# Identity products on TensorE in the first ten slots, and the weights' conversion begun one slot earlier with its last six units late

## The chip, the cores and the metric

The kernel runs on one core of a Trainium2 chip. The metric is the device time of one execution in microseconds (us). The engines are named as in the profile: PE (TensorE: matrix products and transposes), DVE (VectorE), ACT (ScalarE), POOL (GpSimd) and SP (SyncE, which here only issues DMA transfers). Each engine works through its own queue in the order in which the program wrote it.

## The reference

Attention in which every row of scores keeps its 32 largest entries, followed by a two-layer MLP with an exact GELU:

```python
B, H, S, D = 8, 8, 576, 64
scores = q @ k.transpose(0, 1, 3, 2) / sqrt(D)
kth = np.partition(scores, -32, axis=-1)[..., -32:-31]
scores = np.where(scores >= kth, scores, -1e9)
attn = np.exp(scores - scores.max(-1, keepdims=True))
attn = attn / (attn.sum(-1, keepdims=True) + 1e-9)
o = attn @ v                                     # float32
x = o.transpose(0, 2, 1, 3).reshape(4608, 512)
h = x @ w_in                                     # 512 x 2048
out = (0.5 * h * (1 + erf(h / sqrt(2)))) @ w_out # 2048 x 512
```

q, k and v are float32. The weights w_in and w_out lie in memory as 64-bit floats, and the kernel converts them to 32-bit ones itself.

## The kernel before

**Items and slots.** The attention is cut into 144 items. An item is one tile of 128 query rows for a pair of heads (two rows of 576 scores for each partition), or the last 64 query rows of two pairs together. The loop over `n` (line 651) is a software pipeline; one pass of it is called a slot here. Slot `n` issues, in this order: the addition for the weights' unit of the slot (`weights_add`), the scores of item n+2 (`scores`, PE, copied by ACT), the product with v for item n-3 (`attend`, PE; it does something for every second item only), the softmax of item n-1 (ACT, four passes), the transposes of item n-2 (`transposes`: one piece of tails and two main pieces of four transposes, PE, each copied by ACT), the transposes of q and k of coming pairs (`transpose_qk`), the search of the 32 largest for item n (`top_k`, 14 passes of MAX8 and MATCH_REPLACE8 on DVE), the threshold of item n (`threshold`, POOL), the normalising of item n-1 (`normalise`, two passes of POOL or of DVE), the sizing of the next unit of weights (`weights_size`, ACT) and the loads for later slots (SP).

The sum of a softmax row (the denominator) passes from ACT to POOL (`add_small`, line 372) and then to DVE (`inverse`, line 366, at the end of the search of the next item). Its result is what `normalise` needs, and the transposes of the slot after need that.

**MLP.** Its work is cut into pieces (four passes each of 256 columns in the first layer, two of 512 in the second), and `mlp` strews them between the attention's work on PE, 8 in a slot. The first can be issued in slot START = 10, when the first 256 tokens have gone through the attention; slots 10 and 11 take 4 each, later slots 8. What is left after the last slot follows without attention.

**Weights.** There are 16 units of 2 x 128 rows by 512 columns. `load_weights` brings the 64-bit words of a unit with two transfers into a part of `w_out_sb` that is not yet in use, or into a tile of its own (`stage`, lines 154 to 158). `weights_size` makes two passes on ACT (lines 175 and 177) and a third (line 179) that POOL takes over (line 191) for units from slot 12 on; `weights_add` and `weights_end` add on POOL (lines 194 and 206). For units up to slot 10 the second addition stands late in the slot (`ends_late`), behind `add_small`. When a unit's third pass is POOL's, `normalise` goes to DVE in the slot before. Unit i of ORDER is in slot 1 + i, the last one in slot 17:

```python
SLOT_OF = {u: FIRST + i + (i == UNITS - 1) for i, u in enumerate(ORDER)}
```

**PSUM.** The scores have one buffer (`s_ps`). Transposes, the tails of scores and the product with v share a ring of two (`tp`), so PE can't start a piece before ACT has copied the one before the last. A product of zeros runs nine times ahead of the loop (line 630), into the ring of the MLP's first layer.

Of the kernel before, what the change touches and what calls it, by code (L numbers as in the profile page):

```python
# [14 lines left out]
def kernel(  # L15
# [19 lines left out]
    nc = tc.nc  # L35
    f32, i32, u32 = mybir.dt.float32, mybir.dt.int32, mybir.dt.uint32
# [5 lines left out]
    P = 128  # L42
# [19 lines left out]
    ps = ctx.enter_context(tc.tile_pool(name="ps", bufs=2, space=bass.MemoryType.PSUM))  # L62
    ctx.enter_context(tc.manual_schedule())

    ident = const.tile([P, P], f32, name="ident")
# [44 lines left out]
    UNITS = NWI + FT // 2  # L110
# [10 lines left out]


    ORDER = [0, 1, 2, 3, 8, 9, 4, 5, 10, 11, 6, 7, 12, 13, 14, 15]
    FIRST = 1
    START = 2 * NP + 2
    WARM = 9
    words = {}
# [3 lines left out]
    nc.gpsimd.memset(high, EXP0 * 2.0**-21)  # L131


    SLOT_OF = {u: FIRST + i + (i == UNITS - 1) for i, u in enumerate(ORDER)}
    UNIT_IN = {n: u for u, n in SLOT_OF.items()}
    unit_in = UNIT_IN.get

    def load_weights(n, queue=None):

        queue = queue or nc.sync  # L140
        u = unit_in(n)
        if u is None:
            return
        src, r, c, dst = weights_of(u)
        if src.dtype == f32:
            for x in range(2):
                queue.dma_start(
                    out=dst[:, x], in_=src[(r + x) * P : (r + x + 1) * P, c : c + WS]
                )
            return  # L150


        half, i = src.bitcast(u16), ORDER.index(u)
        if i not in (12, 14, 15):
            at = FT // 2 + 4 * (i % 2)
            t = w_out_sb[:, at : at + 4, :].rearrange("p (a b) n -> p a (b n)", a=2)
        else:
            t = stage.tile([P, 2, 2 * WS], f32, tag="words", name="words")
        for a in range(2):
            queue.dma_start(  # L160
                out=t[:, a].bitcast(u16)[:, 0 : 4 * WS - 1],
                in_=half[(r + a) * P : (r + a + 1) * P, 4 * c + 1 : 4 * (c + WS)],
            )
        words[u] = t
# [15 lines left out]

    def on_pool(u):

        return u in words and SLOT_OF[u] >= START + 2

    made = set()

    def weights_add(u):
        if u in words:
            w, _, below, d = parts(u)
            if on_pool(u):  # L190
                nc.gpsimd.tensor_scalar(
                    w.bitcast(i32), w.bitcast(u32), 2.0**-13, None, op0=ALU.mult
                )
            nc.gpsimd.tensor_tensor(d, d, below, op=ALU.add)
            if not ends_late(u):
                weights_end(u)
        made.add(u)

    def ends_late(u):

        return u in words and SLOT_OF[u] <= START

    def weights_end(u):
        if u in words:
            w, _, _, d = parts(u)
            nc.gpsimd.tensor_tensor(d, d, w.bitcast(i32), op=ALU.add)
# [66 lines left out]
    def scores(i):  # L273
        if i >= N:
            return
        pair, t = items[i]
        S_of[i] = s = work.tile([P, 2 * S], f32, tag="s", bufs=5, name="s")
        s_ps = ps.tile([P, 2, 512], f32, tag="s", bufs=1, name="s_ps")
        t_ps = ps.tile([P, 512], f32, tag="tp", name="t_ps")
        if t < NM:  # L280
            qk = qk_of[pair]
            lhsT = qk[:, t * P : (t + 1) * P]
            nc.tensor.matmul(t_ps[:, 0:P], lhsT=lhsT, rhs=qk[:, SM + P : KT], start=True, stop=True)  # L283
            for c in range(2):
                for e in range(2):
                    rows = slice(e * D, (e + 1) * D)
                    nc.tensor.matmul(  # L287
                        s_ps[:, e, c * 256 : (c + 1) * 256], lhsT=lhsT[rows, :],
                        rhs=qk[rows, KT + c * 256 : KT + (c + 1) * 256], start=True, stop=True,
                    )  # L290
            if i == 0:

                nc.scalar.activation(s[:, 0:SM], s_ps[:, 0], func=AF.Copy, scale=scale)  # L293
                nc.vector.tensor_scalar(s[:, SM : S + TL], t_ps[:, 0:P], scale, None, op0=ALU.mult)
                nc.scalar.activation(s[:, S + TL :], s_ps[:, 1], func=AF.Copy, scale=scale)  # L295
                return
            nc.scalar.activation(spread(s, S + TL, SM), s_ps, func=AF.Copy, scale=scale)  # L297
            nc.scalar.activation(s[:, SM : S + TL], t_ps[:, 0:P], func=AF.Copy, scale=scale)
        else:
            for r in range(2):  # L300
                qk = qk_of[pair + r]
                for e in range(2):
                    nc.tensor.matmul(
                        t_ps[half(r, e), r * TL : (r + 1) * TL],
                        lhsT=qk[:, SM + e * TL : SM + (e + 1) * TL],
                        rhs=qk[:, SM + P + e * TL : SM + P + (e + 1) * TL],
                        start=True, stop=True,
                    )

            for r in range(2):  # L310
                qk = qk_of[pair + r]
                for e in range(2):
                    rows = slice(e * D, (e + 1) * D)
                    nc.tensor.matmul(  # L314
                        s_ps[half(r, e), r, :], lhsT=qk[rows, SM + e * TL : SM + (e + 1) * TL],
                        rhs=qk[rows, KT:], start=True, stop=True,
                    )
            s2 = s.rearrange("p (r n) -> p r n", r=2)
            nc.scalar.activation(s2[:, :, 0:SM], s_ps, func=AF.Copy, scale=scale)
            nc.scalar.activation(  # L320
                s2[:, :, SM:S], t_ps[:, 0:P].rearrange("p (r n) -> p r n", r=2),
                func=AF.Copy, scale=scale,
            )
# [116 lines left out]
    def copy_x():  # L440
        while copies:
            copies.pop()()
# [161 lines left out]
    def mlp(n):  # L604
        for _ in range(n):
            if done[0] >= len(pieces) or pieces[done[0]][0] > ready[0] or left[0] == 0:
                return
            pieces[done[0]][1]()
            done[0] += 1
            left[0] -= 1  # L610
            if eager[0]:
                run_gelus()
# [8 lines left out]
    load("k", 1)  # L621
    load("q", 1)
    for n in range(2):
        load_weights(FIRST + n)


    idle = raws["v"][0][:, NM].rearrange("p e d -> p (e d)")
    warm = ps.tile([P, 512], f32, tag="l1", name="warm")
    for _ in range(WARM):
        nc.tensor.matmul(warm[:, 0:P], lhsT=idle, rhs=idle, start=True, stop=True)  # L630
    for pair in range(2):
        for piece in transpose_qk(pair, pair == 0):
            piece()
        if pair == 0:
            scores(0)
            scores(1)

# [11 lines left out]
    for n in range(ahead):  # L651

        left[0] = 4 if n in (START, START + 1) else 8
        eager[0] = n > N
        weights_add(unit_in(n))
        scores(n + 2)
        product = attend(n - 3)
        late = n > START
        if n <= START:

            softmax(n - 1, 0)
        copy_x()
        mlp(1)
        tr = transposes(n - 2)
        if product and n > START and done[0] < len(pieces) and pieces[done[0]][0] > ready[0]:

            for piece in tr[:1]:
                piece()
            tr, ready[0] = tr[1:], n_tok[0]
        if n > START:  # L670
            softmax(n - 1, 0)
        mlp(1)
        if not late:
            softmax(n - 1, 1)
        mlp(1)
        prep = prep_in.pop(n, [])
        if len(prep) > 1 and len(tr) == 3:
            tr, prep = tr[:1] + prep[:1] + tr[1:], prep[1:]
        for piece in tr[:-1]:
            piece()  # L680
            ready[0] = n_tok[0]
            mlp(1)
        ready[0] = n_tok[0]
        if late:
            softmax(n - 1, 1)
        add_small(n - 1)
        if ends_late(unit_in(n)):
            weights_end(unit_in(n))
        for piece in tr[-1:] + prep:
            piece()  # L690
            mlp(1)

        run_gelus()
        mlp(left[0])
        run_gelus()
        if n < N:
            top_k(n, {3: lambda: inverse(n - 1)})
        else:
            inverse(n - 1)
        threshold(n)  # L700
        u = unit_in(n + 1)

        normalise(n - 1, 2 if on_pool(u) else 0)

        weights_size(unit_in(n + 1))
        if n >= FIRST:
            load_weights(n + 2)
        if n <= NP:
            load("v", n)

# [37 lines left out]
```

## Time and profile before

| | |
|---|---|
| Median of 4 runs | 1641.33 us (1639.95 to 1642.26) |
| The profiled execution | 1641.79 us, its span 1640.0 us |
| Busy share of the span | PE 97%, DVE 86%, ACT 72%, POOL 40% |
| Granted PE clock, mean | 0.979 |
| First MAX8 of slots 0, 4, 9, 10, 11, 12 | 11.15, 49.92, 98.43, 108.13, 117.83, 130.16 us |
| DVE's search in one slot of the first ten | 9.7 us |
| DVE waiting for denominators, 108 to 260 us | 11.0 us in 9 waits |

How to read it: the span is the time from the first to the last instruction. The page gives busy time for each engine, and rows of tenths for 40 equal slices of the span (9 is 90% or more); its row PEclk has the share of the full PE clock that was granted. A line of a timeline has the start, the time taken, the engine, the line of the kernel, the operation, what it writes and reads, the count, and in brackets the idle time before it and what ended it. Passes of PE overlap, and the end of each is modelled, so the distance from one start to the next is a better price than the time taken.

### The profile page before, as it was taken

The page shows a single profiled execution, that of the slowest core. Times are in us where ns is not written, and L with a number is a line of the kernel's source. Part 1 is how long each engine was busy: PE and PEld are TensorE (multiplying, and loading weights), DVE is VectorE, ACT ScalarE, POOL GpSimd, SP SyncE. Part 2 cuts the span into 40 slices and gives each one's busy share as a digit, 9 for nine tenths or more (in the row PEclk, how much of TensorE's full clock was granted, in tenths as well). Part 3 has the DMA queues.
Part 4 walks back from the last instruction along what each step waited for, and adds up shares of the span by engine and source line. Part 5 has one row for each costly group of instructions (what it writes and reads, how often), then busy time and mean ns, then how long its engine had stood idle before and what let it go on. Part 6 is the DMA issues. An engine that isn't in the chain of part 4 may idle for free.

```text
span 1640.0 us, 25030 instructions
## 1 busy us (share of the span) xinstructions
PE 1589.4 (97%) x8818; PEld 1076.7 (66%) x8818; DVE 1415.2 (86%) x3046; ACT 1185.6 (72%) x2133; POOL 662.3 (40%) x759
## 2 busy tenths in 40 slices
PE   6669999999999999999999999999999999999999
PEld 4346576766666666676666667676666666666665
DVE  7998999988898989998989898998889888999800
ACT  6999877777777777777777777777777777777720
POOL 4897633333333333333333233333333333333300
PEclk7779999999999999999999999999999999999999
DMA  6433210011101110001100111001110101000000
GB/s 164 139 111 124 55 43 1 14 29 44 35 1 28 30 47 11 10 20 36 30 28 15 29 30 43 1 14 32 41 36 1 28 16 35 1 14 2 6 13 13
DMA packets 126765, 56.14 MB, mean 34 GB/s; under 512 B 117776, under 2 KB 118064, under 8 KB 126640
## 3 DMA queue, kind: packets, MB, share of 16 engines
q1 hardware_dynamic: 125376, 54.12, 12.3%
q8 instruction: 70, 1.15, 0.3%
q10 hardware_dynamic: 1200, 0.39, 0.1%
q14 instruction: 55, 0.45, 0.1%
q0 software_dynamic: 64, 0.03, 0.0%
HBM read 45.08 MB, written 9.44 MB: 33 GB/s over the span
## 4 chain that ended last, share of the span: by engine, by line
PE 91%; ACT 5%; DMA 1%; issue 1%; DVE 1%; POOL 0%; SPq 0%; ACTq 0%; DVEq 0%; POOLq 0%
PE h_ps L518 30%; PE y_ps L554 30%; PE o L466 8%; PE tp L429 8%; PE s_ps L287 7%; PE tp_qk L242 2%; PE t_ps L283 2%; PE o L477 1%; ACT s L380 1%; PE s_ps L314 1%; ACT s L379 1%; PE tp_t L411 1%; ACT w_out_sb L179 1%; ACT s L297 1%; DMA raw_k<-in_k_dram 0%
## 5 line engine op out<-in xcount | busy, mean ns | idle before, releaser
L340 DVE MAX8 top<-rest 128x8 f32<-128x576 f32 x864 | 609.4, 747 | 0.0
L518 PE MATMUL h_ps<-xT,w_in_sb 128*128 128x256 f32 (+1 forms) x2560 | 553.0, 361 | 0.0
L554 PE MATMUL y_ps<-w_out_sb,g 128*128 128x512 f32 x1152 | 548.9, 599 | 0.0
L392 POOL TENSOR_SCALAR s<-s,rden 128x576 f32<-128x576 f32 x278 | 476.5, 1723 | 0.6 <-DVE rden L366 0.4
L518 PEld LDWEIGHTS h_ps<-xT,w_in_sb 128*128 128x128 f32 x2560 | 428.4, 191 | 61.9 <-issue 16.4
L343 DVE MATCH_REPLACE8 rest<-top,rest 128x576 f32<-128x576 f32 x576 | 423.3, 743 | 0.0
L372 POOL TENSOR_SCALAR den<-den 128x2 f32<-128x2 f32 x144 | 32.0, 222 | 837.8 <-ACT s L380 837.5
L554 PEld LDWEIGHTS y_ps<-w_out_sb,g 128*128 128x128 f32 x1152 | 195.1, 190 | 168.2 <-issue 167.3
L297 ACT ACTIVATE s<-s_ps 128x1024 f32<-128x1024 f32 x127 | 130.5, 1027 | 165.2 <-PE s_ps L287 143.5
L380 ACT ACTIVATE s<-s,bias 128x576 f32<-128x576 f32 x288 | 223.4, 776 | 13.2 <-ACT s L379 0.8
L379 ACT ACTIVATE s<-s,neg 128x576 f32<-128x576 f32 x288 | 224.1, 778 | 0.3 <-POOL neg L355 0.2
L436 ACT COPY pt<-tp 128x512 f32<-128x512 f32 x256 | 147.1, 575 | 101.9 <-PE tp L429 101.8
L429 PEld LDWEIGHTS tp<-ident,s 128*128 128x128 f32 x1152 | 145.7, 144 | 101.0 <-issue 58.9
L343 DVE MATCH_REPLACE8 rest<-top,s 128x576 f32<-128x576 f32 x288 | 211.7, 743 | 0.0
L340 DVE MAX8 top<-s 128x8 f32<-128x576 f32 x288 | 201.7, 742 | 1.4 <-ACT s L293 1.4
L429 PE MATMUL tp<-ident,s 128*128 128x128 f32 x1152 | 178.0, 278 | 14.1 <-ACT pt L412 11.7
L466 PE MATMUL o<-pt,raw_v 128*64 128x256 f32 x1280 | 155.7, 390 | 0.0
L287 PE MATMUL s_ps<-qk 64*128 64x256 f32 x1024 | 153.1, 420 | 0.8 <-ACT s L295 0.8
L366 DVE RECIPROCAL rden<-den 128x2 f32<-128x2 f32 x144 | 23.1, 160 | 138.8 <-POOL den L372 138.4
L466 PEld LDWEIGHTS o<-pt,raw_v 128*64 128x64 f32 x1280 | 87.8, 139 | 66.7 <-issue 23.5
L287 PEld LDWEIGHTS s_ps<-qk 64*128 64x128 f32 x1024 | 92.2, 194 | 23.7 <-issue 1.6
L529 ACT ACTIVATE g<-h_ps 128x512 f32<-128x512 f32 x144 | 78.6, 595 | 37.8 <-PE h_ps L518 37.1
(71 smaller groups left out, 1076.1 us busy)
## 6 DMA issues: line engine op xcount, KB each, us to landing
raw_q<-in_q_dram SPq DMA_DIRECT2D x64, 128.0 KB, 2.4
raw_v<-in_v_dram SPq DMA_DIRECT2D x64, 128.0 KB, 2.5
w_out_sb<-in_moe_w_in_dram SPq DMA_DIRECT2D x16, 511.8 KB, 4.8
raw_k<-in_k_dram SPq DMA_DIRECT2D x62, 128.0 KB, 2.5
out_dram<-y SPq DMA_DIRECT2D x31, 256.0 KB, 2.2
w_out_sb<-in_moe_w_out_dram SPq DMA_DIRECT2D x10, 511.8 KB, 4.1
words<-in_moe_w_out_dram SPq DMA_DIRECT2D x6, 511.8 KB, 4.5
out_dram<-y SPq DMA_DIRECT2D x9, 128.0 KB, 2.3
```

Source lines behind the costliest of these rows:

```text
L287: nc.tensor.matmul(s_ps[:, e, c * 256 : (c + 1) * 256], lhsT=lhsT[rows, :], rhs=qk[rows, KT + c * 256 : KT + (c + 1) * 256], start=True, s ...
L297: nc.scalar.activation(spread(s, S + TL, SM), s_ps, func=AF.Copy, scale=scale)
L340: nc.vector.max(st["top"][:, e, 8 * r : 8 * r + 8], cur[e])
L343: nc.vector.match_replace(rest[:, e], st["top"][:, e, 8 * r : 8 * r + 8], cur[e], LOWEST)
L379: nc.scalar.activation(s, s, func=AF.Prelu, bias=st["neg"][:, e, 1:2], scale=1.0, alpha=STEEP)
L380: nc.scalar.activation(s, s, func=AF.Exp, bias=st["bias"][:, e : e + 1], scale=1.0, accum_out=st["den"][:, e : e + 1],)
L392: (nc.vector if e >= 2 - on_dve else nc.gpsimd).tensor_scalar(s, s, st["rden"][:, e : e + 1], None, op0=ALU.mult)
L429: nc.tensor.transpose(tp[:, j * P : (j + 1) * P], s[:, first + j * P : first + (j + 1) * P], ident)
L436: nc.scalar.copy(out=dst, in_=tp.rearrange("p (j n) -> p j n", j=NM))
L466: nc.tensor.matmul(o[e * D : (e + 1) * D, 0:n], lhsT=vt[:, j, e, :], rhs=pt[:, e * NM + j if j < NM else 2 * NM, :], start=(j == 0), stop= ...
L518: nc.tensor.matmul(h_tile(u)[:, i, :], lhsT=w_in_sb[:, ko, f * P : (f + 1) * P], rhs=xT[:, ko, c0 : c0 + n], start=(ko == 0), stop=(ko == ...
L554: nc.tensor.matmul(y_of[sub], lhsT=g_of[u][:, i, sub * P : (sub + 1) * P], rhs=w_out_sb[:, f, :], start=(f == 0), stop=(f == FT - 1),)
```

## The change

Three things are changed. First, `keep_busy` issues products of the identity matrix with itself on PE, whose result nobody reads: in slots 0 to 9, 8 or 28 of them behind the scores (and the product with v), 10 more behind the tails where the slot has a product with v, and 24 at the end of slot 1. Second, unit i of ORDER is in slot i for the first ten; the last six are in slots 11, 13, 14, 15, 16 and 18. The first is sized ahead of the loop, its second addition stands in slot 1 together with that of the second unit, and the third unit's words lie in the tile of their own. Third, all six late units have their third pass on POOL, and the last one is sized in its own slot behind the copy of the product with v.

```diff
-    FIRST = 1
...
-    SLOT_OF = {u: FIRST + i + (i == UNITS - 1) for i, u in enumerate(ORDER)}
+    SLOT_OF = dict(zip(ORDER, [*range(START), 11, 13, 14, 15, 16, 18]))
...
-        if i not in (12, 14, 15):
+        if i not in (2, 12, 14, 15):
...
-        return u in words and SLOT_OF[u] >= START + 2
+        return u in words and SLOT_OF[u] > START
+
+    def waits(u):
+
+        return u == ORDER[-1]
...
-        return u in words and SLOT_OF[u] <= START
+        return u in words and SLOT_OF[u] < START
...
-        load_weights(FIRST + n)
+        load_weights(n)
...
-    warm = ps.tile([P, 512], f32, tag="l1", name="warm")
-    for _ in range(WARM):
-        nc.tensor.matmul(warm[:, 0:P], lhsT=idle, rhs=idle, start=True, stop=True)
+
+    def keep_busy(count, m):
+        warm = ps.tile([P, 512], f32, tag="l1", name="warm")
+        for _ in range(count):
+            nc.tensor.matmul(warm[:, 0:P], lhsT=m, rhs=m, start=True, stop=True)
+
+    keep_busy(WARM, idle)
...
+    weights_size(unit_in(0))
...
-        weights_add(unit_in(n))
+        if not waits(unit_in(n)):
+            weights_add(unit_in(n))
...
         copy_x()
+        if waits(unit_in(n)):
+            weights_size(unit_in(n))
+            weights_add(unit_in(n))
         mlp(1)
...
+        if n < START:
+
+            keep_busy(8 if product or n == 0 else 28, ident)
...
         for piece in tr[:-1]:
             piece()
+            if n < START and product and piece is tr[0]:
+                keep_busy(10, ident)
...
-        if ends_late(unit_in(n)):
-            weights_end(unit_in(n))
+
+        for u in (unit_in(0), unit_in(1)) if n == 1 else (unit_in(n),) if n > 1 else ():
+            if ends_late(u):
+                weights_end(u)
...
+        if n == 1:
+            keep_busy(24, ident)
...
-        weights_size(unit_in(n + 1))
-        if n >= FIRST:
-            load_weights(n + 2)
+        if not waits(unit_in(n + 1)):
+            weights_size(unit_in(n + 1))
+        load_weights(n + 2)
```

## The prediction

> **What bounds the kernel now.** I read the page's clock row and chain of waits first, then the windows view, then the timelines of single engines.
>
> ```profile
> span 1640.0 us, 25030 instructions
> PE   6669999999999999999999999999999999999999
> PEclk7779999999999999999999999999999999999999
> ```
>
> PE is the bound of all but the first three slices, and in these its granted clock is about 0.7. The windows view, cut where the regimes change (columns: stretch, its length, busy time and count of PE, weight loads, DVE, ACT, POOL, then the clock and DMA):
>
> ```profile
> 17.00:54.00 37.00, 22.42 (x88) 14.52 (x86) 37.00 (x79) 32.46 (x51) 26.48 (x23) 0.50 0.52 131
> 11.00:108.00 97.00, 56.45 (x274) 36.57 (x275) 96.85 (x208) 85.52 (x141) 74.08 (x61) 0.69 0.49 145
> 129.50:132.90 3.40, 3.40 (x16) 1.88 (x16) 3.40 (x8) 3.36 (x5) 3.31 (x2) 0.50 0.54 222
> 135.00:1560.00 1425.00, 1424.19 (x8101) 969.17 (x8100) 1289.84 (x2771) 1058.72 (x1928) 558.12 (x666) 1.00 0.10 25
> ```
>
> From 11 to 108 us (slots 0 to 9) DVE never rests: 96.85 of 97.00. From 135 us to the end PE never rests, at full clock. So the end is "the moment at which PE reaches the MLP work of slot 12" (134.31) plus a fixed amount of PE work. A microsecond gained or lost before 134 us reaches the end; later only a PE stall does. Where PE still loses time is its own timeline around slots 9 to 12:
>
> ```profile
> 104.00 0.47 PE L411 MATMUL tp_t<-ident,s 128*128 128x128 f32 x1 [3.65 <-POOL s L392]
> ...
> 114.48 1.03 PE L518 MATMUL h_ps<-xT,w_in_sb 128*128 128x256 f32 x4
> ...
> 118.70 0.60 PE L242 MATMUL tp_qk<-ident,raw_q 128*128 128x128 f32 x4
> 119.14 1.03 PE L518 MATMUL h_ps<-xT,w_in_sb 128*128 128x256 f32 x4
> ...
> 128.88 0.49 PE L283 MATMUL t_ps<-qk 128*128 128x128 f32 x2 [1.39 <-ACT pt L436]
> 129.29 1.96 PE L287 MATMUL s_ps<-qk 64*128 64x256 f32 x8
> 131.19 3.19 PE L466 MATMUL o<-pt,raw_v 128*64 128x256 f32 x20
> ```
>
> The first MLP product is at 114.48; slot 12's scores wait 1.39 for ACT and then run at half clock. What holds the first MLP product is DVE's chain through POOL:
>
> ```profile
> 107.34 2.39 POOL L206 TENSOR_TENSOR w_out_sb<-w_out_sb 128x1024 int32<-128x1024 int32 x1
> 109.71 0.23 POOL L355 TENSOR_SCALAR neg<-top 128x4 f32<-128x4 f32 x1
> 110.02 0.19 POOL L358 TENSOR_TENSOR bias<-neg 128x2 f32<-128x2 f32 x1
> 110.20 3.43 POOL L392 TENSOR_SCALAR s<-s,rden 128x576 f32<-128x576 f32 x2
> ```
>
> DVE ends slot 9 at 108.06, POOL is still adding weights, and slot 8's rows are normalised at 113.63.
>
> **The sum's basis.** The profiled execution took 1641.79 (span 1640.0 and 1.8 around it), 0.46 above the median of 1641.33.
>
> **Part 1, the products.** 8 in slot 0, 28 and 24 in slot 1, 28 each in slots 2, 3, 5, 7, 9, 18 each in 4, 6, 8: 254. One is two passes over 128 columns. At full clock four such passes took 0.44 (118.70 to 119.14), so a product is 0.22; the nine before the loop took 4.21 at half clock, so 0.43 to 0.47 there. That is 56 us at full clock into a stretch where PE idled 97.00 - 56.45 = 40.6 us; the existing work must speed up too. They sit behind the scores and ahead of the transposes, so transposes queue behind them, and ACT's copies behind those.
>
> **Part 2, conversion from slot 0.** A unit costs ACT three rows (1.23, 1.22, 1.13: 3.5 us) and POOL two of 2.40. Slots 1 to 9 keep one each; slot 0 gains one, slot 10 loses its own. Both late additions of units 0 and 1 fall into slot 1, so POOL does 2.4 more there. Now the chain, by rows of before, with the clock full from 20.2 (a 3.4 us stretch of products is past by then):
>
> - Slot 0: ACT sizes unit 0 from 15.8 (words landed 15.3), copies scores(2) by 20.5, one transpose copy, and sizes unit 1 until 25.3 (24.1 before). PE's eight products end at 20.7, its transposes at 21.2.
> - Slot 1, PE: scores 1.4 to 22.6, 28 products 6.1 to 28.7, transposes to 29.4, 24 products 5.2 to 34.6, so scores(4) end at 36.1. ACT: softmax(0) ends 29.7, unit 2 34.1, then 2.0 idle until scores(4). POOL: two additions until 34.9 (31.3 before), normalise until 38.9, unit 2's first addition until 41.3, and only then the denominators of row 1, 41.55. DVE is ready for them at 40.15: a stall of 1.45, where before it had 2.2 to spare.
> - Slot 2: softmax(1) ends 40.5, but the 28 products end at 42.2; ACT begins unit 3 at 45.0 (39.92 before).
> - Slot 3: softmax(2) ends 52.8, denominators 53.1, DVE ready at 51.35: stall 1.75. Slot 4: 0.35. Together DVE is 3.7 late.
> - Slots 5 to 9: per slot DVE 9.7, POOL 9.15, ACT 9.2 to 9.7, PE 1.4 + 6.1 + 1.1 = 8.6 (with attention 8.7). All fit under DVE, which can't catch up: 3.7 stays.
>
> Bounds: without any delay by products DVE would still lose 1.45 to POOL's double addition (nought if softmax(0) ends 1.5 earlier); with slot 1 cold until 23.6 the same chain gives 4.8. I take 3.7, the clock phase of the profiled run. Below nothing is excluded, since DVE had no idle time to give.
>
> **Part 3, slots 10 to 12.** DVE ends slot 9 at 111.8; POOL adds until 112.4, normalises slot 8 by 116.4; the first MLP product is at 116.7, 2.2 late. ACT, with no unit in slot 10 (3.5 us) and PE with no waits there, bring scores(13) to 121.5 (120.00): 1.5 late. Slot 11's unit moves its third ACT row (1.19) to POOL: scores(14) at 129.7 (128.88), 0.8 late. From there to the MLP took 5.43 at half clock (128.88 to 134.31); the same three groups in slot 18 took 3.69 (197.02 to 200.71): 1.74 back if the clock stays full. Between ends 0 and 1.74 I take 1.74, as PE's waits in the 10 us before are 1.4 instead of 2.1. So -0.9.
>
> [...]
>
> **Part 4, the last six units.** Slots 11, 13 to 16, 18; all six now take POOL's multiply (3.10) and put a normalise on DVE (0.95 instead of POOL's 3.43). DVE waited 11.0 us in all for denominators between 108 and 260, so 0.95 more is hidden; its cover gone, 0.95. Slot 12 has POOL normalise row 10 by 136.1, when PE's transposes get there at 136.5: nothing, at worst 1. In slot 18 PE waited 0.72 for POOL (201.73); that row is now DVE's: -0.7. Unit 15's sizing (2.5 on ACT, put ahead of slot 18's softmaxes) makes row 17's normalise end at some 214.4 instead of 212, against transposes at 215.03: hidden, at worst 2. Loads: SP issues a unit's two transfers one slot earlier (0.5 us each), unit 2 at 22 ahead of the first v; the pair issued at 31.35 landed at 37.5, so this one lands by 29 and ACT asks at 30.6; v is read from slot 4 on. If it lands late, its delay adds to the lag.
>
> **Sum:** -0.9 - 0.7 = -1.6, 1641.79 - 1.6 = 1640.2.
>
> **The rivals.** 0.2% (3.3 us) is about what a measurement of this kernel can tell from no change.
>
> - *The early stalls stay small.* DVE loses only POOL's 1.45, or the scores of slot 2 come in time. For it: every early stall above is 0.4 to 2 us, within the error of one chain. Against: 52 products in slot 1 are 11.3 us of work against 9.7. Then slots 10 to 12 give 2.25 more: 1638.0; with no lag at all 1636.5.
> - *The clock sinks among the products* (slower). A 3.4 us stretch at half clock puts 1.7 us into the queue ahead of the transposes, and every softmax end that passes DVE's reciprocal (0.7 to spare in slot 9) becomes DVE's loss. For it: the half clock was granted for 37 us on end, and fell again after waits of 1.4. Against: PE idles about 1 us a slot. Two such stretches and a cold slot 12: 1640.2 + 3.4 + 1.7 = 1645.3. It decides once slot 4's first MAX8 starts after 57 us.
> - *The products don't raise the clock.* 28 at 0.43 are 12 us, a slot 17 instead of 9.7: six such slots and slot 1's 24 more products cost some 50 us, 1690. Against: the clock was full by 7 us, after nine products of zeros.
>
> **How the numbers follow.** Forecast (1638 to 1644.6) 0.43; small stalls 0.30; sinking clock 0.25; no clock 0.02. The range leaves out the no-lag end and the last case: 1636.0 to 1647.0. Faster 0.30, within 0.2% 0.43, slower 0.27. The likeliest case's own range is 1638.2 to 1643.
>
> **What would show it.** Right: clock 1.00 in nearly all of 20 to 110; DVE's reciprocals waiting for POOL's denominators in slots 2 and 3, slot 4's first MAX8 near 53.5 (49.92), slot 10's near 111.8 (108.13); first MLP product near 116.7; slot 12's scores at 1.1 instead of 1.96. Wrong: no DVE wait before 100 us (first rival), a clock of 0.5 after 24 us (second), or PE waits after 140 us, which would mean that a late unit is not hidden.

## The result, and the profile after

The changed kernel takes 1643.02 us (median of 41 runs, 1641.94 to 1645.56), the kernel before 1641.01 us (61 runs, 1639.85 to 1643.9): a ratio of 1.0013, 95% interval 1.0009 to 1.0017. It is 2.0 us slower. That lies within the 0.2% that the prediction called no change, and so many runs can still tell it from none; the forecast had it 0.8 us faster than this median.

The profiled execution of after took 1642.05 us (span 1640.3), that of before 1641.79. So the two traces differ by only 0.26 us, and the rest of the 2.0 is their place among the other runs: before's lies 0.78 above its median, after's 0.97 below its own. The times of after follow the mean granted clock: of the 42 executions listed with their clock (one more than the median counts), 18 with 1.000 have a median of 1642.25 us, 9 with 0.999 of 1643.08, 15 with 0.998 or less of 1644.46, and the trace shows one of the first sort.

The page of after:

```profile
span 1640.3 us, 26040 instructions
PE   8999999999999999999999999999999999999999
PEclk9999999999999999999999999999999999999999
```

The windows view (columns as in the prediction):

```profile
24.00:54.00 30.00, 29.49 (x248) 27.05 (x247) 26.59 (x58) 23.73 (x40) 22.63 (x18) 1.00 0.53 154
11.00:108.00 97.00, 93.16 (x753) 79.80 (x754) 93.06 (x201) 86.70 (x135) 76.25 (x61) 1.00 0.52 155
135.00:1560.00 1425.00, 1424.43 (x8100) 969.00 (x8099) 1292.65 (x2777) 1060.85 (x1928) 559.93 (x666) 1.00 0.10 25
```

The products do what they do on paper: from 11 to 108 us the clock is 1.00 instead of 0.69, and PE is busy for 93.16 us instead of 56.45. But DVE, which had no idle time there, now has some: 93.06 instead of 96.85. From 135 to 1560 us PE's busy time is the same within 0.3 us. The waits of DVE up to 110 us, and its timeline where the first passes of slots 3, 4 and 5 start:

```profile
DVE rden L370 <- POOL den L376: 3.9, 3, 3.1
```

```profile
39.87 0.17 DVE L370 RECIPROCAL rden<-den 128x2 f32<-128x2 f32 x1 [0.34 <-POOL den L376]
...
52.74 0.17 DVE L370 RECIPROCAL rden<-den 128x2 f32<-128x2 f32 x1 [3.06 <-POOL den L376]
52.82 1.40 DVE L344 MAX8 top<-s 128x8 f32<-128x576 f32 x2
...
63.01 0.17 DVE L370 RECIPROCAL rden<-den 128x2 f32<-128x2 f32 x1 [0.46 <-POOL den L376]
```

Three waits for denominators, 3.86 us in all, where before had none. The denominators are late because ACT's softmax is late, and ACT because PE's queue is full of products. ACT's timeline:

```profile
35.14 1.02 ACT L301 ACTIVATE s<-s_ps 128x1024 f32<-128x1024 f32 x1 [2.57 <-PE s_ps L291]
...
41.68 0.27 ACT L416 COPY pt<-tp_t 128x128 f32<-128x128 f32 x1 [2.16 <-PE tp_t L415]
...
44.20 1.25 ACT L175 ACTIVATE w_in_sb<-w_out_sb,low 128x1024 int32<-128x1024 int16 x1
```

and PE's, which is what ACT waits for:

```profile
28.28 5.52 PE L636 MATMUL warm<-ident 128*128 128x128 f32 x48
33.64 0.39 PE L287 MATMUL t_ps<-qk 128*128 128x128 f32 x2
33.96 1.13 PE L291 MATMUL s_ps<-qk 64*128 64x256 f32 x8
35.02 6.52 PE L636 MATMUL warm<-ident 128*128 128x128 f32 x56
41.38 0.27 PE L415 MATMUL tp_t<-ident,s 128*128 128x128 f32 x1
```

The 24 products at the end of slot 1 (48 passes, 28.28 to 33.64) stand ahead of slot 2's scores, and the 28 of slot 2 (35.02 to 41.38) ahead of its transposes. ACT rests 2.57 us for the one and 2.16 for the other, and begins the unit that it sizes in this slot at 44.20, where before began at 39.92.

Then the part in which PE finishes the lead-in, PE's timeline of slots 10 to 12:

```profile
117.52 0.33 PE L415 MATMUL tp_t<-ident,s 128*128 128x128 f32 x1 [1.33 <-POOL s L396]
117.69 1.03 PE L522 MATMUL h_ps<-xT,w_in_sb 128*128 128x256 f32 x4
...
122.46 0.38 PE L287 MATMUL t_ps<-qk 128*128 128x128 f32 x2
...
130.83 0.49 PE L287 MATMUL t_ps<-qk 128*128 128x128 f32 x2 [1.39 <-ACT pt L440]
131.25 1.13 PE L291 MATMUL s_ps<-qk 64*128 64x256 f32 x8
132.31 2.38 PE L470 MATMUL o<-pt,raw_v 128*64 128x256 f32 x20
134.62 1.56 PE L522 MATMUL h_ps<-xT,w_in_sb 128*128 128x256 f32 x6
```

The first MLP product starts 3.21 us later than before, slot 12's scores 1.95 later; they then run at full clock (1.13 instead of 1.96), and the MLP of slot 12 starts at 134.62, 0.31 later than before. In slot 16 the distance grows to 1.01, in slot 18 it shrinks to 0.10, and from 209 us on PE stands 0.26 later.

### The profile page after: what moved, and what is told of

The parts are those of the page before. It is cut to its first block, busy times and chain, and to the rows that moved or that the text cites. A ratio compares the mean times of both kernels' runs of the same rounds, so it can differ in the third digit from the quotient of the medians.

```text
span 1640.3 us, 26040 instructions
## 1 busy us (share of the span) xinstructions
PE 1625.1 (99%) x9326; PEld 1120.7 (68%) x9326; DVE 1416.2 (86%) x3048; ACT 1186.8 (72%) x2132; POOL 662.2 (40%) x758
## 4 chain that ended last, share of the span: by engine, by line
PE 93%; ACT 3%; POOL 2%; issue 1%; DMA 1%; DVE 0%; ACTq 0%; POOLq 0%; SPq 0%; DVEq 0%
PE h_ps L522 31%; PE y_ps L558 31%; PE o L470 8%; PE s_ps L291 8%; PE tp L433 7%; PE tp_qk L246 2%; PE t_ps L287 2%; PE warm L636 1%; PE o L481 1%; POOL s L396 1%; PE tp_t L415 1%; PE s_ps L318 1%; ACT s L384 1%; ACT s L383 0%; ACT w_out_sb L179 0%
## 5 line engine op out<-in xcount | busy, mean ns | idle before, releaser
L433 PE MATMUL tp<-ident,s 128*128 128x128 f32 x1152 | 173.0, 273 | 0.9 <-ACT pt L416 0.7
L470 PE MATMUL o<-pt,raw_v 128*64 128x256 f32 x1280 | 152.3, 384 | 0.0
L291 PE MATMUL s_ps<-qk 64*128 64x256 f32 x1024 | 145.2, 402 | 0.8 <-ACT s L299 0.8
L291 PEld LDWEIGHTS s_ps<-qk 64*128 64x128 f32 x1024 | 88.1, 186 | 22.0 <-ACT s L299 1.0
```

The source lines that it names most:

```text
L291: nc.tensor.matmul(s_ps[:, e, c * 256 : (c + 1) * 256], lhsT=lhsT[rows, :], rhs=qk[rows, KT + c * 256 : KT + (c + 1) * 256], start=True, s ...
L433: nc.tensor.transpose(tp[:, j * P : (j + 1) * P], s[:, first + j * P : first + (j + 1) * P], ident)
L470: nc.tensor.matmul(o[e * D : (e + 1) * D, 0:n], lhsT=vt[:, j, e, :], rhs=pt[:, e * NM + j if j < NM else 2 * NM, :], start=(j == 0), stop= ...
```

## The experiments

All were run in five rounds beside the kernel before, in groups; within a group the runs of before are the same. The ratios are to the kernel before, with 95% intervals.

| run | median us | ratio | profiled us | DVE's waits for denominators, slots 2 on |
|---|---|---|---|---|
| after | 1643.02 | 1.0013 [1.0009, 1.0017] | 1642.05 | 0.34, 3.06, 0.46 |
| e1: no products in the loop | 1641.46 | 1.0003 [0.9994, 1.0012] | 1641.36 | 0.54, 0, 1.14 |
| e2: products alone | 1643.75 | 1.0016 [1.0007, 1.0025] | 1643.75 | 0, 2.74, 0.76 |
| e3: products from slot 4 | 1641.90 | 1.0004 [0.9995, 1.0012] | 1642.15 | 0, 0, 1.92, 1.79 |
| e4: without the 24 | 1639.39 | 0.9993 [0.9984, 1.0002] | 1638.57 | 0.22 |
| e12: the same again | 1640.00 | 0.9995 [0.9986, 1.0004] | 1638.47 | 0.7 in two |
| e5: e4, a unit in slot 12 | 1640.23 | 0.9996 [0.9987, 1.0005] | 1639.88 | 0.6 in two |
| e7: 12 for the 24 | 1640.36 | 0.9995 [0.9986, 1.0004] | 1640.17 | 1.42, 0, 0.46 |
| e8: the 24, but none in slot 2 | 1644.31 | 1.0022 [1.0012, 1.0032] | 1646.58 | 1.33, 0.97, 3.52, 1.31 |
| e9: e5, slot 9's addition late | 1640.50 | 0.9994 [0.9986, 1.0003] | 1641.11 | 1.40, later 0.89 |
| e10: e4, one addition in slot 1 | 1639.28 | 0.9990 [0.9981, 0.9999] | 1640.04 | one of 0.8 |
| e11: e10, slot 9's addition late | 1638.65 | 0.9988 [0.9979, 0.9997] | 1637.77 | 1.0 in two |
| e13: e11, six products in slot 11 | 1644.56 | 1.0028 [1.0017, 1.0038] | 1643.52 | 1.2 in two |

### Which part costs: weights alone, products alone

The first experiment takes all products out of the loop of after; the second puts them into the kernel before and leaves the weights where they were.

```diff
 # e1, against after
-        if n < START:
-            keep_busy(8 if product or n == 0 else 28, ident)
...
-            if n < START and product and piece is tr[0]:
-                keep_busy(10, ident)
...
-        if n == 1:
-            keep_busy(24, ident)
```

> The changed kernel without any product of the identity; the weights' new slots stay. Theory A (the products of slots 1 to 3 queue ahead of the scores and transposes, ACT gets late and DVE stalls; POOL's doubled addition costs a smaller stall): DVE waits for denominators before 100 us fall from 3.9 to 0.5 to 1.5 us, slot 10's first MAX8 comes near 109.5 instead of 111.8, but slots 9 to 12 run partly at half clock again; about 1641.5, 1 to 2 us under the changed kernel. Theory B (the weights' part is what costs): as slow as the changed kernel, 1643, or slower. Theory C (the late units cost after slot 10): PE waits above 1 us after 140 us, and the time of the changed kernel.

> The kernel before with the products of the changed one, weights' units where they were. Theory A: DVE waits of 2 to 3 us for denominators in slots 2 to 4, full clock in slot 12, nothing given back by an empty slot 10; 1642.5 to 1644.5. Theory B: the products are harmless, 1639.5 to 1641, faster than before by the 1.7 us of slot 12's clock.

The weights alone make no difference that 11 runs show (1.0003), the products alone cost 2.6 us (1643.75 against 1641.14 of the kernel before, measured with it). Both times lie where theory A put them. The trace of e2 has DVE's wait at the same place as after, without any second addition of POOL in slot 1:

```profile
51.86 0.17 DVE L366 RECIPROCAL rden<-den 128x2 f32<-128x2 f32 x1 [2.74 <-POOL den L372]
```

So the large wait is the products' and not that of the weights' order. Both kernels pay something: e1 runs from 11 to 108 us at a clock of 0.69 as before did, and waits 1.14 in slot 4.

### The 24 products at the end of slot 1

```diff
 # e4 (and e12), against after
-        if n == 1:
-            keep_busy(24, ident)
```

> The changed kernel without the 24 products at the end of slot 1. Theory A: ACT's idle 2 us ahead of slot 2's scores go, the DVE wait in slot 3 falls from 3.06 to about 1 us; 1641 to 1641.5, 2 us under the changed kernel. Theory B: 1643, unchanged, and the wait in slot 3 stays.

> The kernel without the 24 once more, beside these two: 1639 to 1640.

1639.39 and 1640.00 when measured twice, 3.0 to 3.6 us below after and below the 1641 to 1641.5 that was expected. ACT's and PE's timelines of e4:

```profile
31.78 1.18 ACT L179 ACTIVATE words<-words 128x1024 int32<-128x1024 uint32 x1
32.85 1.00 ACT L301 ACTIVATE s<-s_ps 128x1024 f32<-128x1024 f32 x1
...
37.84 0.27 ACT L416 COPY pt<-tp_t 128x128 f32<-128x128 f32 x1 [0.63 <-PE tp_t L415]
```

```profile
127.36 0.49 PE L287 MATMUL t_ps<-qk 128*128 128x128 f32 x2 [1.39 <-ACT pt L440]
...
131.16 2.86 PE L522 MATMUL h_ps<-xT,w_in_sb 128*128 128x256 f32 x12
```

The scores' copy follows the weights on ACT with no rest (32.85, where after waited 2.57 and began at 35.14), and the wait for the transposes is 0.63 instead of 2.16. DVE loses 0.22, the MLP of slot 12 starts at 131.16, 3.46 before that of after, and the profiled run is 3.48 shorter. DVE's waits are 3.64 shorter, and its search of slot 10 begins at 108.37 instead of 111.77, 3.40 earlier: what DVE loses in slots 2 to 4 reaches the end nearly one to one. Without the 24 the clock is 1.00 from 11 to 108 us too, and its mean over the profiled execution 1.000, so they bought nothing that this trace shows.

Half of them:

```diff
 # e7, against after
-            keep_busy(24, ident)
+            keep_busy(12, ident)
```

> The changed kernel with 12 products at the end of slot 1 instead of 24 (2.6 us instead of 5.2). Theory D (what counts is by how much the products outlast ACT's conversion of unit 2, 2.57 us in the changed kernel's profile): 12 fit nearly whole into that time, DVE waits before 100 us stay at 0.2 to 0.8, about 1639.5, as without any. Theory E (every product in the early queue costs its time, in proportion): half of the loss, DVE waits near 2 us, 1641.2.

With 12 slot 3's wait is gone, as theory D said. The time of 1640.36 lies between the two expectations, and it is not told from the kernel without them. Its wait of 1.42 in slot 2 stands in a trace whose clock was half from 15.9 to 19.4 (mean 0.999, in e4 1.000); there softmax(0) ends at 29.30 instead of 27.95, and POOL's second addition is no longer covered.

### Other places for the early products

> The changed kernel with the products of slots 4 to 9 alone (none in 0 to 3, none of the 24). Theory A: DVE waits before 100 us 0.5 to 1.5, slot 10 near 109.5, full clock from about 57 us through slot 12; 1639.5 to 1641, some 2.5 us under the changed kernel. Theory B: 1643.

```diff
 # e3, against after, which also leaves out the 24
-        if n < START:
+        if 3 < n < START:
```

> The changed kernel with the 24, but without the 28 products of slot 2. Theory D': the 24 and the 28 stand in one queue ahead of slot 2's transposes, so leaving out either takes the transposes off the path: DVE waits before 100 us fall to about 1 us, 1639.5 to 1640.5. Rival: the 24 cost through the late scores of slot 2 alone: the 2.57 us that ACT waits for them stay, and so do DVE waits of 3 us and the 1643.

```diff
 # e8, against after
-        if n < START:
+        if n < START and n != 2:
```

Both expectations of e8 missed, and e3 fell outside its own. e3 waits no less than after, only later (1.92 and 1.79 in slots 4 and 5). Its windows say at what clock it came there:

```profile
20.90:41.30 20.40, 9.63 (x40) 6.23 (x37) 20.34 (x45) 17.90 (x30) 15.36 (x12) 0.50 0.77 220
44.80:58.40 13.60, 9.59 (x41) 6.22 (x43) 13.60 (x31) 11.83 (x20) 12.58 (x9) 0.50 0.28 69
```

Slot 4's product with v takes 4.12 us there (54.85 to 58.89 on PE) instead of 2.38. The products of slot 4 stand behind it, the last 10 of them from 60.89 to 63.12, ahead of the main transposes. ACT's timeline of e3 separates the two:

```profile
59.04 0.37 ACT L475 COPY xT<-o 128x256 f32<-128x256 f32 x1 [0.84 <-PE o L470]
...
63.76 1.07 ACT L440 COPY pt<-tp 128x512 f32<-128x512 f32 x2 [2.40 <-PE tp L433]
```

Slot 4's wait of DVE ends with softmax(3), at 60.99, and up to there ACT has waited for nothing that stands behind a product; this wait comes with PE's work at half clock, as in e1, which has no products and waits 1.14 us in the same slot. Slot 5's wait ends with softmax(4), at 72.58, and ahead of that ACT rests 2.40 us for transposes behind the 10 products. e8 shows what the second rival priced, a clock that sinks ahead of products. Its windows, and PE's timeline:

```profile
25.00:39.00 14.00, 11.21 (x98) 10.41 (x96) 14.00 (x30) 11.26 (x19) 10.95 (x9) 1.00 0.67 189
39.00:49.00 10.00, 8.76 (x36) 7.10 (x37) 8.67 (x21) 8.57 (x14) 9.75 (x8) 0.50 0.60 180
```

```profile
37.89 0.33 PE L415 MATMUL tp_t<-ident,s 128*128 128x128 f32 x1 [2.45 <-POOL s L396]
...
43.45 2.08 PE L291 MATMUL s_ps<-qk 64*128 64x256 f32 x8
45.45 8.32 PE L636 MATMUL warm<-ident 128*128 128x128 f32 x56
53.62 0.27 PE L415 MATMUL tp_t<-ident,s 128*128 128x128 f32 x1
```

Where slot 2's products were, PE now waits 2.45 for POOL and 1.42 for ACT; at 39.0 the clock falls, the scores take 2.08, and slot 3's 28 products take 8.17 us (45.45 to 53.62) instead of 6.36. DVE waits 3.52 in slot 4 and 7.1 in all. In after, slot 2's products do two things at once: they keep the clock up (1.00 from 24 to 54 us, where e8 has 0.50 from 39 to 49), and they delay the transposes.

### POOL's additions, and where the best kernel is

```diff
 # e10, against e4: unit 0's second addition stays in slot 0
-        for u in (unit_in(0), unit_in(1)) if n == 1 else (unit_in(n),) if n > 1 else ():
-            if ends_late(u):
-                weights_end(u)
+        if ends_late(unit_in(n)):
+            weights_end(unit_in(n))
```

```diff
 # e11, against e10 (e9 does the same to e5)
-        if ends_late(unit_in(n)):
+        if n != START - 1 and ends_late(unit_in(n)):
             weights_end(unit_in(n))
...
         normalise(n - 1, 2 if on_pool(u) else 0)
+        if n == START - 1:
+            weights_end(unit_in(n))
```

> As with the unit in slot 12, and slot 9's second addition on POOL behind the normalise instead of ahead of it. PE's wait of 1.3 us for the normalise in slot 10 goes and the first MLP product comes near 113 instead of 114.2. If PE is then the bound at once: 1 us below the kernel with the unit in slot 12, 1637 to 1638. Rival: DVE's pace holds slot 12 (its normalise follows slot 11's search, which nothing here moves): same time as that kernel.

> Without the 24, and unit 0's second addition in slot 0, so that slot 1 has one on POOL instead of two. Three profiles with two additions there showed DVE waiting 1.4 us at the end of slot 2 whenever the early clock was at half, and 0.2 when it was full. If the doubled addition is the cause: no wait there in any phase, the median 0.5 to 1.3 us under that without the 24 alone, 1638.2 to 1639. Rival (the half clock alone is the cause): 1639.4 and the wait stays.

> As the kernel before it, and slot 9's second addition behind the normalise; the late units as in the changed kernel. First MLP product 4.5 us after slot 10's first MAX8 instead of 5.9, slot 12's scores 0.9 us earlier: 1637.4 to 1638.4. Rival: DVE's pace takes it back by slot 12, the time of the kernel before it.

e10 measured beside e12: 1639.28 against 1640.00, with intervals that overlap, so the doubled addition's price is not told apart from nothing in the time. In the traces it is, as far as they have products in slots 0 and 1: with two additions in slot 1, DVE waits 1.33 to 1.42 us in slot 2 where the clock was half for a stretch between 15 and 20 us (e7, e8, e9) and 0.19 to 0.35 where it was full (after, e4, e5, e12); with one addition it does not wait there in either case (half in e11 and e13, full in e10). Slot 9's addition has a clear mechanism in the trace. POOL's timeline of e11:

```profile
108.51 0.23 POOL L359 TENSOR_SCALAR neg<-top 128x4 f32<-128x4 f32 x1 [0.84 <-DVE rden L370]
...
108.99 3.43 POOL L396 TENSOR_SCALAR s<-s,rden 128x576 f32<-128x576 f32 x2
112.39 2.42 POOL L210 TENSOR_TENSOR w_out_sb<-w_out_sb 128x1024 int32<-128x1024 int32 x1
```

POOL now waits for DVE instead of DVE's result waiting for POOL, PE's 1.33 us wait for the normalised rows is gone, and the first MLP product starts 4.45 us after slot 10's first MAX8 (112.85 against 108.40); in e10 it is 5.89. e11 has the lowest median of the case: 1638.65, 0.9988 [0.9979, 0.9997] of the kernel before, and 4.4 us under after. Its interval overlaps with that of e10, so what the last edit is worth in time is not shown, and the median lies 0.25 above the range that was expected. e9, with the same edit on e5, isn't told from e5 and missed its 1637 to 1638; its trace has the half clock from 129.0 on and so loses in slot 12 what it gained in slot 10.

### Two attempts that gained nothing

A unit in slot 12 instead of 11, to free ACT ahead of slot 12's scores:

```diff
 # e5, against e4
-    SLOT_OF = dict(zip(ORDER, [*range(START), 11, 13, 14, 15, 16, 18]))
+    SLOT_OF = dict(zip(ORDER, [*range(START), 12, 13, 14, 15, 16, 18]))
```

> Without the 24, and the first late unit in slot 12 instead of 11, so that slot 11's softmaxes no longer have its 2.5 us of ACT ahead of them. If that unit is what makes PE wait 1.4 us for ACT ahead of slot 12's scores: that wait goes, 1638.0 to 1638.8. If the wait is only exchanged for one in slot 12 or 13 (rival): 1639.4, as without the 24 alone.

The rival was right. PE's timeline of e5:

```profile
127.66 0.49 PE L287 MATMUL t_ps<-qk 128*128 128x128 f32 x2 [1.39 <-ACT pt L440]
...
137.37 0.66 PE L433 MATMUL tp<-ident,s 128*128 128x128 f32 x4 [0.78 <-ACT pt L416]
```

The wait of 1.39 stays, and the sizing, now ahead of slot 12's softmax, holds up the copy of the tails: a new wait, and the first product of the MLP's second layer at 142.05 instead of 140.75.

Six products in slot 11, to hold the clock through slot 12:

```diff
 # e13, against e11
             mlp(1)
...
+        if n == START + 1:
+            mlp(left[0])
+            keep_busy(6, ident)
         run_gelus()
```

> The best kernel so far (no 24 products, one POOL addition in each of slots 0 and 1, slot 9's second addition behind the normalise; median 1638.65) with six products of the identity at the end of slot 11, where PE waits 1.4 us for ACT ahead of the scores of slot 12. Theory: the clock falls in slot 12 in some executions because PE idles in slots 10 and 11, and six products (6 x 0.22 = 1.3 us) fit into that wait; the scores, the product with v and the first MLP group of slot 12 then always take 3.8 us, not 5.4, and the median is 0.3 to 0.8 lower, 1637.9 to 1638.4, with a narrower spread of runs. Rival: the four passes of the MLP that are drawn ahead of the products and the products themselves stand in front of work that somebody waits for, and what is filled is not what lets the clock fall: the scores of slot 12 start 0.3 to 1 later, median 1638.7 to 1639.5.

5.9 us slower than e11, which neither side had foreseen. PE's timeline and ACT's:

```profile
129.56 2.93 PE L636 MATMUL warm<-ident 128*128 128x128 f32 x12 [3.77 <-ACT g L533]
132.28 0.48 PE L287 MATMUL t_ps<-qk 128*128 128x128 f32 x2
```

```profile
127.61 1.28 ACT L533 ACT_TABLE_LOAD   x1
128.91 1.09 ACT L533 ACTIVATE g<-h_ps 128x512 f32<-128x512 f32 x2
```

The products write into the ring of the MLP's first layer. In slots 0 to 9 it is empty; in slot 11 its buffers hold results that ACT has yet to read with the GELU, behind a table load. PE stands still for 3.77 us (1.39 at this place in e11) for a buffer to which it will write what nobody wants, and the six products run at half clock: 2.7 us (129.56 to 132.28) instead of 1.3. `mlp(left[0])` drew nothing ahead here: the same MLP work stands before the products as in e11.

## Why the prediction was right and wrong

The chain was the right one, and what it gave can be set against the trace point by point:

| step | forecast | measured |
|---|---|---|
| clock from 11 to 108 us | 1.00 nearly throughout | 1.00 |
| 24 products; 28 products | 5.2; 6.1 us | 5.36; 6.36 |
| DVE's stalls in slots 2, 3, 4 | 1.45, 1.75, 0.35 | 0.34, 3.06, 0.46 |
| slot 10's first MAX8 | 111.8 | 111.77 |
| POOL's addition in slot 9 ends | 112.4 | 113.55 |
| first MLP product | 116.7 | 117.69 |
| scores(13) | 121.5 | 122.46 |
| scores(14) | 129.7 | 130.83 |
| from there to the MLP of slot 12 | 3.69 | 3.79 |
| slot 18's wait of PE | -0.7 | gone, but 0.7 lost in slot 16 |
| sum | -1.6 | +0.26 |

**Right: the clock, the price of a product, and the lag, this with some luck.** Three early stalls were forecast as 3.55 us together (1.45, 1.75 and 0.35; the sum took 3.7) and came to 3.86. Their split was wrong and didn't matter: softmax(0) ended at 27.95 instead of 29.7, so POOL's double addition no longer held DVE up for 1.45. The wait in slot 2 was 0.34, with POOL ready at 39.42 and softmax(1) ending last at 39.52. DVE came to slot 3's denominators earlier and waited there the longer. What sets DVE's return is the end of softmax(2), forecast for 52.8, measured 52.4; a stall ahead of it is not added to it. That slot 10 began at the forecast time was in part luck: DVE's first search began at 10.44 instead of 11.15, 0.71 earlier than in before, and the four slots 2 to 5 together took 4.36 longer, not 3.7. The double addition's 1.4 appears only in traces with a stretch of half clock before 20 us (e7, e8, e9).

**Wrong: "POOL adds until 112.4, normalises slot 8 by 116.4; the first MLP product is at 116.7, 2.2 late".** This is the larger of the two terms that turned the sign of the profiled difference. I moved DVE's end of slot 9 by its lag and let POOL catch up: in before the addition ended 1.65 us after DVE, and I let it end 0.6 after. But POOL's denominators wait for ACT's softmax, which had no idle time to catch up either: ACT's copy of the tails in slot 9, which follows its softmax, went from 106.86 to 110.70, later by 3.84 as DVE is by 3.64. POOL's timeline of before, first line, and of after:

```profile
107.04 0.22 POOL L372 TENSOR_SCALAR den<-den 128x2 f32<-128x2 f32 x1 [0.72 <-ACT s L380]
...
110.89 0.22 POOL L376 TENSOR_SCALAR den<-den 128x2 f32<-128x2 f32 x1 [0.94 <-ACT s L384]
111.19 2.39 POOL L210 TENSOR_TENSOR w_out_sb<-w_out_sb 128x1024 int32<-128x1024 int32 x1
113.55 0.23 POOL L359 TENSOR_SCALAR neg<-top 128x4 f32<-128x4 f32 x1
```

POOL already waited 0.72 us for ACT in before and waits 0.94 in after, so it had time to spare and could not use it. The addition begins behind that and ends 1.84 after DVE (113.55 against 111.71). The 1.15 us stay in the later rows of the table (1.0, 1.0, 1.1) and are 1.2 at the MLP of slot 12, at 134.62 instead of 133.4. e11 shows the addition's part the other way round: moved behind the normalise, it brings the first MLP product 1.44 us nearer to DVE's search than in e10.

**Wrong: "that row is now DVE's: -0.7".** Slot 18's wait is gone, as said, and PE makes up 0.9 us there. But slot 16, where before sized no unit, now has one on ACT ahead of its scores (177.62 to 180.08), and PE, 0.31 late until then, waits in that slot and leaves it 1.01 late:

```profile
184.62 0.66 PE L433 MATMUL tp<-ident,s 128*128 128x128 f32 x4 [0.48 <-ACT pt L416]
```

I had costed the moved sizing for slot 18 and not for 16. The two terms, 1.2 and 0.7, make the 1.9 us between -1.6 and +0.26. No experiment took this unit out of slot 16; its 0.7 is read from the two traces alone.

**The clock in slot 12.** 1.74 back was right in the profiled run (3.79 instead of 5.43). I chose that value because PE's waits ahead of it are shorter, and that reason is not borne out: e9 and e10 had PE waits of 1.39 and 1.33 and less, no longer than after's, and fell to half at 129.0 and 127.4. The value was right for this execution and the reason for it was not, so it came out by luck. After's clock held in slot 12 and that of e9 and e10 did not, so the row was rightly left between two ends.

**Left out: the spread about one execution.** The sum ran from a profile 0.78 above before's median to one kind of run of after, and after's other executions, with a lower mean clock, take longer (above). A chain whose time goes with the granted clock (a median of 1642.25 us at a mean clock of 1.000, of 1644.46 at 0.998 or less) has a distribution, and the forecast priced one member of it. Of the 2.82 us between 1640.2 and the median 1643.02, 0.97 is this and 1.86 are the two terms above. The range, said to leave out the case with no lag (1636.5), begins at 1636.0 and holds it; that changed nothing here.

**The rivals.** Small early stalls: not in after, but close to what remains without the 24 (DVE's wait 0.22; 1638.57 profiled, where the rival's sum was 1638.0). The clock sinking among the products: not in after, whose slot 4 starts at 52.82 with the clock full; e8 shows it, with a clock of 0.50 from 39.0 us, at 1644.31, near the rival's 1645.3. That the products don't raise the clock: excluded by after's page.

**What stays open.** What the double addition in slot 1 and the late one in slot 9 cost over many runs, since e12, e10 and e11 overlap from one to the next; and when the clock falls in slots 11 and 12.

## What to carry to other kernels

Filler work on an in-order engine is free only up to the gap it fills: 28 products fitted into a slot's wait, 24 more ahead of the next scores made ACT, and through it DVE, wait and cost 3 us or more. When a lag is passed down a chain of engines that are all near full, it moves every engine's work, so shift all of them and look for an order of instructions that lets one engine's late work go behind what others wait for, as POOL's addition in slot 9. And a filler needs an output buffer: ask who has to free it.

## What the runs showed of the hardware

In e10 the granted clock fell where PE's longest wait since 115 us was 1.39 us; the windows view:

```profile
120.00:124.00 4.00, 4.00 (x22) 3.26 (x19) 4.00 (x11) 3.91 (x7) 3.92 (x2) 1.00 0.36 79
124.00:127.40 3.40, 1.77 (x14) 1.30 (x13) 3.40 (x8) 2.90 (x7) 2.96 (x3) 1.00 0.71 177
127.40:130.80 3.40, 3.40 (x16) 1.98 (x18) 3.40 (x9) 3.37 (x5) 1.94 (x3) 0.50 1.02 408
```

In the 3.4 us ahead of the fall PE was busy for 1.77 us, and the stretch of half clock is 3.4 us long, as that of before (129.50 to 132.90). The same wait of 1.39 us stands in after, e4 and e11, whose scores behind it run at full clock: 1.13, 1.14 and 1.13 us, where e10's take 2.08.

No limit on PE's busy time follows from this. In before PE was busy for 1.67 us of the 3.4 from 126.00 to 129.40, and from 129.50 the clock was 0.50; in after it was busy for 1.67 us of the 3.3 from 128.00 to 131.30, and the clock stayed at 1.00. In before the 3.4 us from 74.85 and from 95.33, with PE busy for 1.82 and 1.80, had the full clock as well. What decides between the two is not shown by these runs.
